# Retention attention and two MLPs on one core: a longer run of loads in flight, and one turn's matmuls in another order

## The chip, the cores and the metric

The kernel runs on one core of one Trainium2 chip. The metric is the device time of one execution in microseconds (us): the median over several runs, lower is better. A profiled execution of the same program gives the trace from which all rows below come; its times count from the start of its span.

## The reference: what is computed

Three stages follow each other. The input has batch 4, 8 heads, 576 positions and 64 features a head.

```python
scores = scale * np.matmul(q, k.transpose(0, 1, 3, 2))
Dmat = np.where(rel >= 0, gamma[:, None, None] ** rel[None, :, :], 0.0)   # causal decay, one rate a head
x = np.matmul(scores * Dmat, v)            # then (tokens, heads*64): 2304 x 512
...
h = x @ w_in;  g = np.maximum(h, 0.0) + alpha * np.minimum(h, 0.0)
x = g @ w_out                              # 512 -> 2048 -> 512
...
h = x @ w2_in; g = h * (1.0 / (1.0 + np.exp(-1.702 * h)))
out = g @ w2_out                           # 512 -> 2048 -> 512
```

## The kernel before, in words

**Attention** takes the heads in 16 pairs (4 batches by 4 pairs of heads), one pair a turn of the loop over `i`, 17 turns in all. A pair needs 1728 columns of 128 partitions in float32 (tile `ld`: queries, keys, values) and 512 columns of the keys in their other layout (tile `kts`). One column of 128 partitions is 512 bytes, so a pair is 2240 columns or 1.15 MB. The positions go in blocks of 128: products within a block (`a_scores` into PSUM tile `sc`, masked and decayed by VectorE in `a_evac`, then `a_within` with the values into PSUM tile `av`), and states that carry the decayed sum of outer products of keys and values from block to block (`a_outer` and `a_tail` into PSUM tile `st`, `a_states` on ScalarE, `a_sums` on VectorE, `a_across` into `av`). `a_keys` scales the keys of the next pair on ScalarE. In turn `i` TensorE computes the scores, the outer products and the tail of pair `i`, and the products with the values (`a_within`, `a_across`) of pair `j = i - 1`. The tile `av` has two buffers; `a_rests` on VectorE (a line of the helper `sub`, L109) is the last reader of a buffer before it is used again.

**Loads.** All loads of attention are issued by SyncE (SP), which works strictly in order. `a_load(i + 4)` stands at the end of turn `i`; `ld` has five buffers. Between them stand the loads of the first MLP's weights, which come as rows `m` of 1 MB, each in two pieces of 1024 columns (0.52 MB, tile `raw`): the rows 0, 1 and 2 lie between the loads of attention, rows 3, 4 and 5 behind them. Every one of these loads goes through `paced`: before it is issued, it waits for the landing of an earlier load, the latest one from which on at least `FLYING` columns have been issued. The unit is one column.

```python
for other, n in reversed(flying):
    behind += n
    if behind >= FLYING:
        tc.add_manual_dep(ins.ins, other.ins.name, SYNC, reason="transfers on their way")
        break
```

Each load signals its landing on one of eight semaphores, DMAHW0 to DMAHW7, which are handed out in turn; a wait on a semaphore is a wait for the load that had it last.

**The weights** are 64-bit words that are turned into float32 on chip: `w_sat` (L150), `w_range` (L154) and `w_top` (L158) on ScalarE, `w_low` (L165) on VectorE, then each is split into a high and a low part (`w_hi` L104, `w_lo` L109). A list of times (`at`, `run_to`) says in which turn each of these instructions is put into its engine's queue; the queues then run in order, so an instruction that waits for a piece of weights holds up what stands behind it on its engine.

**The first MLP** (`mm1` L532 into `h`, `mm2` L573 into `acc`) begins right behind attention, and **the second** (L714) behind it. Every product is made of three matmuls over high and low parts.

Of the kernel before, what the change touches and what calls it, by code (L numbers as in the profile page):

```python
# [39 lines left out]
NG = 5  # L40
SUM = {1: 0, 2: 1, 4: 2, 5: 3}
RING = ("w6", "X1", "w15", "X2", "X4")
FLYING = 2300
HOME = (0, 7, 2, 3, 4, 5, 6, 15)


# [1 line left out]
def kernel(  # L48
# [68 lines left out]
    def run_to(time):  # L117
        while events and events[0][0] <= time:
            _, _, fn, args = events.pop(0)
            fn(*args)  # L120
# [9 lines left out]
    def paced(out, in_, size):  # L130
        ins = nc.sync.dma_start(out=out, in_=in_)  # L131
        behind = 0
# [4 lines that stand above are left out]
# [213 lines left out]
    def a_tables(p):  # L350
        def table(o, c0, n, row, key):
            nc.vector.scalar_tensor_tensor(
                out=tab_sb[o, p, c0:c0 + n], in0=row, scalar=vtab_sb[o, p, key:key + 1],
                in1=mask_sb[o, o.start:o.start + n], op0=ALU.mult, op1=ALU.mult,
            )

        for e in range(2):
            table(slice(0, 128), e * 128, 128, query(p, e), e)
        for e, o in enumerate(halves):
            table(o, 256, 64, query(p, e, o, 64), 4)  # L360

    def a_otab(p):
        for e, o in enumerate(halves):
            copy(tab_sb[o, p, 320:448], query(p, e, o))
        o = tab_sb[:, p, 320:768]
        copy(o[:, 128:256], o[:, 0:128])
        copy(o[:, 256:448], o[:, 0:192])

    def mm(out, lhsT, rhs, start, stop):
        return nc.tensor.matmul(  # L370
            out=out, lhsT=lhsT, rhs=rhs, start=start, stop=stop, skip_group_check=True
        )

    def a_keys(i):
        n = kts(i).rearrange("p (j n) -> p j n", j=4)
        for e, o in enumerate(halves):
            scale(n[:, :, o], n[:, :, o], vtab_sb[:, PAIRS[i][1], e:e + 1])
        k_t[i] = n

    def a_scores(i, chunks=range(4)):  # L380
        q, k = ld[i][0:2]
        if i not in sc_t:
            sc_t[i] = [aps.tile([128, 512], F32, tag="sc", name="sc", bufs=3) for _ in halves]
        t = sc_t[i]
        for j in chunks:
            for h in halves:
                for e, o in enumerate(halves):
                    mm(t[e][h, j * 128:j * 128 + 128], k[j][o, h], q[j][o], j == 0, True)

    def a_tail(i):  # L390
        q, k = ld[i][0:2]
        for o in halves:
            mm(s_t[i][o, 0:64], k[4][o], q[4][o], i == 0, True)

    def a_outer(i):
        t, v, n = s_t[i], ld[i][2], k_t.pop(i)
        for j in range(4):
            for e, o in enumerate(halves):
                mm(t[o, j * 64 + 64:j * 64 + 128], n[:, j, o], v[:, 2 * j + e], i > 0 and j == 0, True)

    def a_evac(i):
        for e, t in enumerate(sc_t.pop(i)):
            nc.vector.tensor_tensor(  # L403
                out=r_t[i][0][:, e].rearrange("p (j n) -> p j n", j=4),
                in0=t.rearrange("p (j n) -> p j n", j=4),
                in1=tab_sb[:, PAIRS[i][1], e * 128:e * 128 + 128].rearrange(
                    "p (a n) -> p a n", a=1).to_broadcast([128, 4, 128]),
                op=ALU.mult,
            )

    def a_queries(i):
        behind = latest[0]
        r = tmp("r", i, [128, 2048])
        r_t[i] = (
            r[:, 0:1024].rearrange("p (e n) -> p e n", e=2), r[:, 1024:1536],
            r[:, 1088:1600].rearrange("p (b n) -> p b n", b=2)[:, :, 0:64], r[:, 1600:2048],
        )
        ins = nc.gpsimd.tensor_tensor(
            out=r_t[i][3], in0=ld[i][3], in1=tab_sb[:, PAIRS[i][1], 320:768], op=ALU.mult
        )  # L420
        if behind:
            tc.add_manual_dep(ins.ins, behind.ins.name, SYNC, reason="beside the products of the scores")

    def a_states(i):
        p = PAIRS[i][1]
        s = r_t[i][1]
        scale(s[:, 0:320], s_t.pop(i)[:, 0:320], vtab_sb[:, p, 2:3])

    def a_sums(i):
        p = PAIRS[i][1]  # L430
        s = r_t[i][1]
        nc.vector.scalar_tensor_tensor(
            out=s[:, 320:512], in0=s[:, 64:256], scalar=vtab_sb[:, p, 2:3], in1=s[:, 128:320],
            op0=ALU.mult, op1=ALU.add,
        )
        half = r_t[i][2]
        nc.vector.scalar_tensor_tensor(
            out=s[:, 384:512].rearrange("p (b n) -> p b n", b=2), in0=half,
            scalar=vtab_sb[:, p, 3:4], in1=s[:, 384:512].rearrange("p (b n) -> p b n", b=2),
            op0=ALU.mult, op1=ALU.add,  # L440
        )
        latest[0] = nc.vector.tensor_tensor(
            out=s[:, 0:64], in0=s[:, 0:64], in1=tab_sb[:, p, 256:320], op=ALU.mult
        )

    def a_within(i):
        v, r = ld[i][2], r_t[i][0]
        t = aps.tile([128, 1024], F32, tag="av", name="av", bufs=2)
        av_t[i] = t, [t[:, A0 + j * 128:A0 + j * 128 + 128] for j in range(4)] + [t[:, A0 + 512:A0 + S]]
        for j in range(4):  # L450
            for e, o in enumerate(halves):
                mm(av_t[i][1][j][o], v[:, 2 * j + e], r[:, e, j * 128:j * 128 + 128], j % 2 == 0, True)

    def a_across(i):
        out, v = av_t[i][1], ld[i][2]
        _, s, _, q = r_t.pop(i)
        for c in range(1, 5):
            s0 = 64 if c == 1 else 192 + c * 64
            for o in halves:
                mm(out[c][o], s[o, s0:s0 + 64], q[o, c * 128 - 128:min(c * 128, 448)], False, True)  # L460
        for o in halves:
            mm(out[4][o], v[o, 8], s[o, 0:64], False, True)

    def a_out(i):
        b, p = PAIRS[i]
        t = av_t.pop(i)[0][:, A0:A0 + S]
        ld.pop(i)
        s0 = 0
        for c in range(2):
            n0, n1 = max(CH[c][0] - b * S, 0), min(CH[c][1] - b * S, S)  # L470
            if n0 >= n1:
                continue
            if (c, p) not in x_t:
                x_home(c, p, xp[c])
            o = b * S - CH[c][0]
            x = x_t[c, p][:, :, n0 + o:n1 + o]
            copy(x[:, 0], t[:, n0:n1])
            rests.append((x, t[:, n0:n1]))
            s0 = n1
        if s0 < S:  # L480
            n = i - NP
            if n // 3 not in xs_t:
                xs_t[n // 3] = tmp("xs", n // 3, [128, 3, S])
            copy(xs_t[n // 3][:, n % 3, s0:S], t[:, s0:S])
# [3 lines left out]
    def a_rests():  # L488
        while rests:
            x, t = rests.pop(0)  # L490
            sub(nc.vector, x[:, 1], t, x[:, 0])
# [452 lines left out]
    with tc.manual_schedule():  # L944
# [24 lines left out]
        for i in range(n_a + 1):  # L969
            j = i - 1  # L970
            if i < n_a:
                a_scores(i)
                a_queries(i)
                a_evac(i)
            if i in (1, 2):
                a_tables(i + 1)
            a_rests()
            run_to(i)
            if i < n_a:
                s_t[i] = aps.tile([128, 512], F32, tag="st", name="st")  # L980
                if i == 0:
                    a_tail(i)
                a_outer(i)
                if i == 0:
                    a_states(i)
                    a_tables(1)
            if i != 1:
                a_within(max(j, 0))
            if 0 < i < n_a:
                a_tail(i)  # L990
                a_states(i)
            if i < n_a:
                a_sums(i)
            if i + 1 < n_a:
                a_keys(i + 1)
            if i == 0:
                a_otab(1)
            run_to(i + 0.25)
            if i:
                a_across(j)  # L1000
                a_out(j)
            if i in (1, 2):
                a_otab(i + 1)
            for n in (3, 4) if i == 0 else (i + 4,):
                if n < n_a:
                    a_load(n)
            if i == 0:
                nc.sync.dma_start(out=alpha_sb, in_=alpha)
            run_to(i + 0.75)
# [173 lines left out]
```

## Time and profile before

| | us |
|---|---|
| median of 3 runs | 815.01 |
| lowest and highest | 814.62, 815.68 |
| the profiled execution, its own time | 813.96 |
| its span in the trace | 812.3 |
| busy time of TensorE in it (98%) | 795.7 |
| mean granted TensorE clock, share of full speed | 0.995 |

The span is what the trace shows from the first to the last instruction; 1.66 us of the profiled execution's own time lie around it. Attention takes the first 79.7 us, the first MLP begins there. TensorE is busy nearly all of the time; "busy" covers slow matmuls too, so the places to look at are the waits.

### The profile page before, as it was taken

The numbers are of one execution on the slowest core, as the hardware profiler recorded it, in microseconds if no ns is written. First come the engines' busy times: TensorE is split into PE (matmuls) and PEld (weight loads), VectorE is DVE, ScalarE is ACT, GpSimd is POOL, SyncE is SP. The second block draws the span as 40 slices with busy tenths as digits, with TensorE's granted clock in tenths as the row PEclk, the third lists the DMA queues.
The fourth block names the chain that finished last, engine by engine and source line by source line (L and its number), as shares of the span: only waits on it lengthen the run. The fifth ranks groups of instructions, "written<-read, shape, count | busy, mean of one in ns | idle before, by whom it ended". The sixth has DMA issues, their size and how long they took to land.

```text
span 812.3 us, 14660 instructions
## 1 busy us (share of the span) xinstructions
PE 795.7 (98%) x5260; PEld 740.2 (91%) x5260; DVE 643.2 (79%) x1195; ACT 528.1 (65%) x959; POOL 82.3 (10%) x104
## 2 busy tenths in 40 slices
PE   8879999999999999999999999999999999999998
PEld 7767788888888888899999999999999999999998
DVE  6757897889765676878998899799787799777775
ACT  6557977888454676546577767666566676566553
POOL 2322120100001211534300000000000000000000
PEclk9989999999999999999999999999999999999999
DMA  8989999876579987598899756987544986446881
GB/s 288 317 281 324 368 322 355 329 284 234 197 263 363 398 287 248 166 316 307 277 370 333 257 161 203 336 303 261 160 120 138 358 291 222 145 122 211 290 274 64
DMA packets 89663, 214.11 MB, mean 264 GB/s; under 512 B 8179, under 2 KB 44019, under 8 KB 80886
## 3 DMA queue, kind: packets, MB, share of 16 engines
q1 hardware_dynamic: 82656, 187.99, 66.1%
q0 software_dynamic: 6784, 25.17, 9.1%
q8 instruction: 41, 0.67, 0.3%
q14 instruction: 32, 0.26, 0.1%
q10 hardware_dynamic: 150, 0.02, 0.0%
HBM read 152.59 MB, written 60.56 MB: 262 GB/s over the span
## 4 chain that ended last, share of the span: by engine, by line
PE 87%; DMA 10%; ACT 2%; SPq 1%; DVE 0%; issue 0%; DVEq 0%
PE acc L714 32%; PE h L714 25%; PE acc L573 15%; PE h L532 14%; DMA raw<-in_w_dram 5%; DMA ld<-in_qkv_dram 3%; DMA kts<-in_kn_dram 1%; SPq L131 0%; ACT raw L150 0%; ACT raw L158 0%; ACT gsf L104 0%; ACT g L545 0%; DVE raw L195 0%; DVE r L403 0%; ACT raw L154 0%
## 5 line engine op out<-in xcount | busy, mean ns | idle before, releaser
L109 DVE TENSOR_TENSOR gsf<-g,gsf 128x384 fp32r<-128x384 f32 (+1 forms) x272 | 157.0, 590 | 54.2 <-ACT gsf L104 53.0
L104 ACT ACTIVATE gsf<-g 128x384 fp32r<-128x384 f32 (+1 forms) x272 | 145.8, 542 | 74.7 <-PE acc L714 33.0
L573 PE MATMUL acc<-gsf,wo 128*128 128x512 f32 x576 | 138.5, 390 | 0.9 <-ACT gsf L104 0.6
L532 PE MATMUL h<-x,wi 128*128 128x512 f32 x576 | 138.2, 389 | 0.0
L714 PE MATMUL acc<-gsf,ws 128*128 128x384 f32 x768 | 135.0, 334 | 0.0
L714 PEld LDWEIGHTS acc<-gsf,ws 128*128 128x128 f32 x768 | 133.3, 188 | 0.0
L573 PEld LDWEIGHTS acc<-gsf,wo 128*128 128x128 f32 x576 | 107.9, 188 | 24.5 <-ACT gsf L104 1.0
L532 PEld LDWEIGHTS h<-x,wi 128*128 128x128 f32 x576 | 108.0, 188 | 22.5
L714 PE MATMUL acc<-x,ws 128*128 128x384 f32 x660 | 128.2, 334 | 0.0
L714 PEld LDWEIGHTS acc<-x,ws 128*128 128x128 f32 x660 | 115.6, 188 | 0.0
L714 PE MATMUL h<-x,ws 128*128 128x384 f32 x540 | 107.7, 334 | 0.0
L714 PE MATMUL h<-gsf,ws 128*128 128x384 f32 x576 | 101.8, 334 | 0.0
L714 PEld LDWEIGHTS h<-gsf,ws 128*128 128x128 f32 x576 | 100.0, 188 | 0.0
L714 PEld LDWEIGHTS h<-x,ws 128*128 128x128 f32 x540 | 94.8, 188 | 0.0
L195 DVE TENSOR_TENSOR tm<-h,tm 128x384 f32<-128x384 f32 x97 | 53.7, 554 | 26.9 <-PE h L714 21.5
L195 DVE TENSOR_TENSOR g<-g 128x384 f32<-128x384 f32 x114 | 63.3, 555 | 0.7
L540 DVE SCALAR_TENSOR_TENSOR g<-g,rise_sb,h 128x512 f32<-128x512 f32 (+1 forms) x49 | 36.4, 743 | 31.7 <-ACT g L545 31.5
L104 ACT ACTIVATE tm<-acc 128x384 f32<-128x384 f32 x62 | 30.4, 491 | 47.4 <-PE acc L714 45.8
L545 ACT ACTIVATE g<-h 128x512 f32<-128x512 f32 (+1 forms) x49 | 29.0, 592 | 39.8 <-PE h L532 39.2
L195 DVE TENSOR_TENSOR raw<-raw 128x256 f32<-128x256 f32 x116 | 45.7, 435 | 1.0
L150 ACT ACTIVATE raw<-raw 128x1024 f32<-128x1024 f32 x32 | 36.5, 1141 | 14.4 <-DMA raw<-in_w_dram 11.0
L165 DVE SCALAR_TENSOR_TENSOR raw<-raw 128x1024 int32<-128x1024 int32 x32 | 39.4, 1231 | 2.7 <-ACT raw L158 2.6
(104 smaller groups left out, 915.8 us busy)
## 6 DMA issues: line engine op xcount, KB each, us to landing
ws<-sm SPq DMA_DIRECT2D x32, 1024.0 KB, 6.8
ws<-sp SPq DMA_DIRECT2D x24, 1024.0 KB, 5.5
raw<-in_w_dram POOLq DMA_DIRECT2D x44, 512.0 KB, 7.9
sm<-raw SPq DMA_DIRECT2D x32, 512.0 KB, 4.3
pad<-rg SPq DMA_DIRECT2D x48, 256.0 KB, 2.7
ld<-in_qkv_dram SPq DMA_DIRECT2D x26, 432.0 KB, 4.7
raw<-in_w_dram SPq DMA_DIRECT2D x20, 512.0 KB, 7.4
r<-raw SPq DMA_DIRECT2D x16, 512.0 KB, 3.0
```

The costliest lines, as they stand in the source:

```text
L104: return nc.scalar.activation(out=out, in_=in_, func=ACTF.Copy)
L109: latest[0] = eng.tensor_tensor(out=out, in0=a, in1=b.bitcast(F32), op=ALU.subtract)
L150: nc.scalar.activation(out=f, in_=f, func=IDENTITY_SAT240, scale=2.0 ** -9)
L165: latest[0] = nc.vector.scalar_tensor_tensor(out=g[:, 0:2 * DM], in0=t[:, :, 1], scalar=3, in1=t[:, :, 0], op0=ALU.logical_shift_left, op1 ...
L195: latest[0] = (eng or nc.vector).tensor_tensor(out=out, in0=x, in1=y, op=op)
L532: nc.tensor.matmul(out=t, lhsT=w[:, cw, k * 128:k * 128 + 128], rhs=x[:, cx], start=(i == 0), stop=(i == 3 * NK - 1),)
L540: nc.vector.scalar_tensor_tensor(out=g[0], in0=g[1], scalar=rise_sb[:, m:m + 1], in1=h, op0=ALU.mult, op1=ALU.add)
L545: nc.scalar.activation(out=out, in_=in_, func=ACTF.Relu, scale=-1.0)
L573: nc.tensor.matmul(out=acc[0][d], lhsT=w[:, d // 2, cw, d % 2 * 128:d % 2 * 128 + 128], rhs=g[:, cx], start=(m == m0 and i == 0), stop=(m ...
L714: nc.tensor.matmul(out=out, lhsT=w(cw), rhs=x(cx), start=(start and n == 0), stop=True, skip_group_check=True,)
```

## The change

`FLYING` goes from 2300 columns (1.18 MB) to 3500 (1.79 MB). In the fourth turn (`i == 3`) the products of pair 2 with its values (`a_within`) are put ahead of the outer products of pair 3.

```diff
-FLYING = 2300
+FLYING = 3500
...
                 if i == 0:
                     a_tail(i)
+                if i == 3:
+                    a_within(j)
                 a_outer(i)
                 if i == 0:
                     a_states(i)
                     a_tables(1)
-            if i != 1:
+            if i not in (1, 3):
                 a_within(max(j, 0))
             if 0 < i < n_a:
                 a_tail(i)
```

On SP no load is moved; what changes is the load for which each one waits. This is the stretch around the two pieces of row 1 of the weights (`raw_577`), with the second half of pair 10 (the second `ld_641`); the numbers tell tiles apart. Before:

```order
L131 DMA raw_577<-in_w1_dram 128x1024 [waits DMAHW0_49]
L131 DMA ld_641<-in_qkv_dram 128x864 [waits DMAHW2_49,PE_49,Pool_49]
L131 DMA kts_126<-in_kn_dram 128x512 [waits DMAHW3_49,Activation_49]
L131 DMA ld_641<-in_qkv_dram 128x864 [waits DMAHW4_49]
L131 DMA raw_577<-in_w1_dram 128x1024
L131 DMA ld_708<-in_qkv_dram 128x864 [waits DMAHW1_49,DMAHW6_49,PE_49,Pool_49]
```

And the same loads with the change:

```order
L131 DMA raw_577<-in_w1_dram 128x1024 [waits DMAHW7_49]
L131 DMA ld_641<-in_qkv_dram 128x864 [waits DMAHW0_49,PE_49,Pool_49]
L131 DMA kts_126<-in_kn_dram 128x512 [waits DMAHW1_49,Activation_49]
L131 DMA ld_641<-in_qkv_dram 128x864 [waits DMAHW2_49]
L131 DMA raw_577<-in_w1_dram 128x1024 [waits DMAHW3_49]
L131 DMA ld_708<-in_qkv_dram 128x864 [waits DMAHW4_49,PE_49,Pool_49]
```

DMAHW4 is the semaphore of the first piece of `raw_577`, DMAHW2 and DMAHW3 those of the two loads ahead of it (`kts` and the second half of `ld` of pair 9). So the second half of pair 10 waited for the piece of weights, with 864 + 512 = 1376 columns (0.70 MB) issued behind that piece; now it waits for the `kts` of pair 9, with 864 + 1024 + 864 + 512 = 3264 columns (1.67 MB) issued behind it. Among loads of attention alone it was 2240 columns (1.15 MB), and is 2752 or 3104 (1.41 or 1.59 MB).

On TensorE the fourth turn reads so (`st<-ld,kts` are the outer products, `av<-r,ld` the products with the values):

```order
 L370 MATMUL sc<-ld 64x128 x16
-L370 MATMUL st<-ld,kts 64x64 x8
-L370 MATMUL av<-r,ld 64x128 x8
+L370 MATMUL av<-r,ld 64x128 x8
+L370 MATMUL st<-ld,kts 64x64 x8
 L370 MATMUL st<-ld 64x64 x2
```

The eight products with the values of pair 2 stand ahead of the eight outer products of pair 3; nothing else moves on any engine.

## Rows read from the trace of the kernel before

**Rows 1.** The page: its first line.

```profile
span 812.3 us, 14660 instructions
```

**Rows 2.** Waits of TensorE over the run: us in total, times, longest.

```profile
PE sc L370 <- DMA ld<-in_qkv_dram: 6.7, 7, 2.0
PE st L370 <- ACT kts L334: 2.8, 1, 2.8
...
PE acc L573 <- ACT gsf L104: 0.6, 1, 0.6
...
PE acc L573 <- ACT raw L104: 0.4, 1, 0.4
```

**Rows 3.** The chain that ended last, in order of time: start, us, what.

```profile
39.83 5.96 DMA raw<-in_w_dram
...
66.77 4.06 DMA ld<-in_qkv_dram
...
70.88 0.74 PE sc L370 x16
...
77.41 9.62 DMA raw<-in_w_dram
...
100.59 2.97 PE acc L573 x12
```

**Rows 4.** Waits of SP's queue, 0 to 80 us: us in total, times, longest.

```profile
SPq L131 <- DMA ld<-in_qkv_dram: 21.4, 24, 2.6
SPq L131 <- DMA kts<-in_kn_dram: 16.0, 15, 2.5
SPq L131 <- DMA raw<-in_w_dram: 9.2, 6, 2.6
```

**Rows 5.** Windows: busy time by engine; last three columns: clock, DMA share, GB/s.

```profile
10.00:20.00 10.00, 9.46 (x220) 8.17 (x218) 8.29 (x21) 7.89 (x24) 2.44 (x3) 1.00 0.95 314
2.00:51.00 49.00, 42.15 (x886) 35.87 (x885) 33.43 (x78) 29.15 (x70) 11.41 (x10) 0.99 0.92 309
...
2.00:71.00 69.00, 57.87 (x1226) 49.74 (x1229) 45.30 (x104) 43.80 (x97) 17.16 (x15) 0.95 0.91 305
80.00:110.00 30.00, 29.06 (x126) 23.07 (x125) 23.96 (x38) 27.36 (x38) 2.29 (x4) 1.00 1.01 372
44.00:48.00 4.00, 3.35 (x74) 2.79 (x72) 3.38 (x7) 1.37 (x4) 1.14 (x1) 1.00 0.76 230
```

**Rows 6.** Timeline of SP's queue, 42 to 46 us: start, us, what.

```profile
42.64 0.58 SPq L131 DMA_DIRECT2D kts<-in_kn_dram  x1
45.81 0.33 SPq L131 DMA_DIRECT2D ld<-in_qkv_dram  x1
```

**Rows 7.** Timeline of TensorE: pieces of attention that waited, wait in brackets.

```profile
34.40 0.67 PE L370 MATMUL sc<-ld 64*64 64x128 f32 x16 [1.00 <-DMA ld<-in_qkv_dram]
...
39.85 0.67 PE L370 MATMUL sc<-ld 64*64 64x128 f32 x16 [1.34 <-DMA ld<-in_qkv_dram]
...
53.34 1.41 PE L370 MATMUL st<-ld,kts 128*64 128x64 f32 x15 [2.80 <-ACT kts L334]
...
68.83 0.67 PE L370 MATMUL sc<-ld 64*64 64x128 f32 x16 [0.55 <-DMA ld<-in_qkv_dram]
70.88 0.67 PE L370 MATMUL sc<-ld 64*64 64x128 f32 x16 [1.39 <-DMA ld<-in_qkv_dram]
```

**Rows 8.** Timeline of ScalarE around 51 us.

```profile
51.38 1.10 ACT L150 ACTIVATE raw<-raw 128x1024 f32<-128x1024 f32 x1 [6.00 <-DMA raw<-in_w_dram]
```

**Rows 9.** Timeline of TensorE in the fourth turn.

```profile
18.48 0.69 PE L370 MATMUL st<-ld,kts 128*64 128x64 f32 x16
19.71 1.09 PE L370 MATMUL av<-r,ld 128*64 128x128 f32 x16 [0.54 <-DVE x L109]
```

**Rows 10.** Timeline of TensorE in the first MLP.

```profile
88.76 3.29 PE L573 MATMUL acc<-gsf,wo 128*128 128x512 f32 x12 [0.57 <-ACT gsf L104]
```

**Rows 11.** Line L131 (the paced loads), 0 to 72 us: issue to landing.

```profile
DMA to landing us min/median/max: 2.7/4.7/6.2
```

## The prediction

> **What bounds the kernel now.** I began with the waits of TensorE over the whole run [rows 2]. They fall into two places. Nearly all stand in attention: 6.7 us for the scores' operands to land and 2.8 us for keys that ScalarE had not yet scaled. Behind attention only 0.6 and 0.4 us are left, both where the first MLP begins. From there on nothing stops TensorE, so whatever is won or lost by 100 us should reach the end unchanged. That confines the question to the first eighth of the span [rows 1].
>
> The chain that ended last says what sets that part. It reaches TensorE's unbroken work at 100.59 us and before that goes through transfers: the load of pair 14's second half, issued at 66.77 and landed 4.06 us later, releases the scores at 70.88; a piece of weights issued at 77.41 takes 9.62 us to land and feeds the first MLP [rows 3]. The reader should see that in between stands SP: each load was issued when another had landed. SP's own waits confirm it: 21.4 + 16.0 + 9.2 = 46.6 us in which it held a load back for an earlier one [rows 4]. The pacing by columns is such a wait.
>
> Then the windows, for whether the 16 DMA engines had work meanwhile. From 2 to 71 us they were busy 0.91 of the time at 305 GB/s; from 80 to 110 us, where many transfers are on their way, 1.01 at 372 GB/s; from 10 to 20 us, where the stream has no weights in it yet, 0.95 [rows 5]. So while the core waits for transfers, the engines idle 69 x 0.09 = 6.2 us.
>
> The timelines show where. In the stretch quoted with the change, SP issues `kts` at 42.64 and the next load only at 45.81 [rows 6], when the piece of weights issued at 39.83 has landed, at 45.79 [rows 3]. Only 0.70 MB had been issued behind that piece. The window 44 to 48 us falls to a share of 0.76 and 230 GB/s [rows 5]: 0.96 us of idle engines. The weights bring six such pieces into the stream, which are the six waits for `raw` in SP's list [rows 4].
>
> **The change part by part.**
>
> *The pacing.* It adds no instruction and no byte and moves no load. It shortens the holds. In front of the load that is awaited there were 2240 columns among attention's loads and 1376 behind a piece of weights; now 2752 to 3264, at both places more than in the best of the old stretches. What is that worth? The stretch from 2 to 71 us holds 69 x 0.91 = 62.8 us of work for the engines. The least gain is none, if the idle share comes from something else than the holds. At 0.95, the share of 10 to 20 us with 2240 columns in front, it would last 66.1 us: 2.9 us less. At 1.0 it would last 62.8: 6.2 us less. I take 0.96, close to the row with the same sort of loads and a little above it, because more stands in front than there: 62.8 / 0.96 = 65.4, so the load of pair 14 lands **3.6 us** earlier. I leave the rate per busy engine as it is (305 / 0.91 = 335 GB/s), though the later stretch shows 368.
>
> A page can be held against this. The hole at 44 to 48 us shows 0.96 us lost behind 0.70 MB, and 10 to 20 us shows 0.05 of the time lost behind 1.15 MB [rows 5]. The Trainium skill, DMA: Bandwidth & Descriptors (Anatomy of one DMA), gives a transfer a fixed part of about 2.0 us, most of it the receipt of the last write, and beyond it bytes over 436 GB/s, fitted on transfers issued by GpSimd. By that page 0.70 MB cover 1.6 us of the 2.0 and leave 0.4 us, six times 2.4 us, and 1.15 MB leave nothing; its estimate of the gain is 2.4 us. The trace agrees on the kind, and shows more idle time at both depths.
>
> *Whether TensorE can follow.* Pair 14 waited 0.55 + 1.39 = 1.94 us for its two halves [rows 7]; without them it would have been ready at 70.88 - 1.94. What held it further up is in turn 10: ScalarE stood 6.00 us at 51.38 for the second piece of weights row 1 [rows 8], the scaling of the keys was queued behind, and the outer products waited 2.80 us for that, to 53.34 [rows 7]. That piece also moves: the window 2 to 51 us, 49 us at 0.92 [rows 5], gives 49 x (1 - 0.92 / 0.96) = 2.0 us. So TensorE can follow by 1.94 + 2.0 = 3.9 us, just more than the 3.6 us that the load gives. At a share of 1.0 the two bounds are 6.2 and 49 x 0.08 + 1.94 = 5.9 us; the latter is the upper bound of the gain.
>
> *Behind attention.* At 70.88 the scores release VectorE, which releases stores and then SP's next loads, up to the weights' piece of 77.41 [rows 3]. All of that is counted from 70.88 and moves with it. The engines are full there, so the 9.62 us stay. In the first MLP TensorE waited 0.57 us for work queued behind that piece on ScalarE [rows 10], so this landing has to move as far as attention does; I take that it does. The bound below is that it does not move, and then only the 0.57 and 0.4 us of waiting are gained.
>
> *The fourth turn.* Eight outer products (0.69 us) stood between the scores and the products with the values, and these still waited 0.54 us for the last reader of their `av` buffer on VectorE [rows 9]. Turned round, the products with the values start at the same 19.71, since VectorE sets that, and the outer products follow instead of filling the wait: at most 0.69 us later. If the scaled keys of pair 3 came late the turn would save something, but before they were ready by 18.48. What covers the 0.69 us is TensorE's later waits for loads: 1.00 us at 34.40 and 1.34 at 39.85 [rows 7]. With loads 38 x (1 - 0.92 / 0.96) = 1.6 us earlier by then, 2.34 - 1.6 = 0.74 us of wait is left, just enough. Price: nothing; 0.69 us if the loads get faster than I take, and then it lies in the part that the 6.00 us of ScalarE sets anyway.
>
> *Sum.* 0 for the order, -3.6 us for the pacing. The profiled execution took 813.96 us, of which 812.3 are span [rows 1]; 813.96 - 3.6 = 810.4. It lies 1.05 us below the median of the runs, 815.01, to which the forecast is made: **811.4 us**.
>
> **The rivals.**
>
> *The engines are fuller, the bytes no faster.* The idle share may come from slow packets or from engines that finish unevenly, so that the slowest has no idle time now and more in front adds only queueing. For it: from 10 to 20 us, with steady depth, 0.95 still gave only 314 GB/s [rows 5], hardly more than the mean of 305. Against it: the clear hole behind the weights' piece and the 372 GB/s with more on the way. Then no landing moves: 815.0.
>
> *Won in attention, given back at the first MLP.* The piece of weights of 77.41 needs 9.62 us in a stretch where the engines are full [rows 3]. If that stretch is bound by its bytes from further back than SP's issue, it lands when it did, and TensorE waits longer at 88.76. Gain 0.57 + 0.4 us [rows 2, 10]: 814.0. Against it: before 80 us the engines still had gaps.
>
> *Slower: what is needed now shares the engines with what is needed later.* If transfers on their way divide the bandwidth and don't land in the order of their issue, more of them make each one later. Landing took 4.7 us in the median with about 2240 + 864 columns on the way [rows 11]; with 3104 + 864 it takes 4.7 x 3968 / 3104 = 6.0. The chain has two such landings that decide, pair 14's and the weights' piece behind it, so 2 x 1.3 = 2.6 us: 817.6. It decides once the longer landing exceeds what the earlier issue gives, 1.3 us each. For it: the 9.62 us of the piece where most is on its way [rows 3]. Against it: in that same stretch the rate is the best of all [rows 5], and 4.7 us is about the time that everything in front takes, which tells nothing of the order. On the page named above, Latency and other measured facts lets the access of HBM go from 0.2 us to 2 us under high load, which would make landings later too; no run here shows it by itself.
>
> **How the numbers follow.** About 0.2% (1.6 us) is what a measurement of this kernel can tell from no change. Forecast (0.96, down to 0.95 and up to full engines): 0.66. No faster bytes: 0.17. Given back: 0.08. Slower: 0.09. The forecast's own range is 815.0 - 5.9 = 809.1 to 815.0 - 2.9 = 812.1. The two cases without a change have 0.25 together, so the range must take them in: up to 815.2, and down to 809.0. The slower case stays outside. Faster by over 0.2% (under 813.4) is the forecast alone, 0.66; the same, 0.25; slower, 0.09.
>
> **What would show it.** Right: the share of the DMA engines from 2 to 71 us rises to 0.95 or more; no gap of 3 us in SP's issues behind a piece of weights; the scores of pair 14's second half start at about 67.3 instead of 70.88; the piece of weights for the first MLP lands near 83.4; TensorE's unbroken work begins near 97. In the fourth turn the products with the values wait about 1.2 us and start near 19.7. Wrong: a higher share at the same 305 GB/s, or pair 14 still at 70 us; landings of 6 us with later scores in the first turns; a wait of 3 to 4 us in place of the 0.57 at the first MLP; or a new wait of ScalarE or SP for buffers that takes the place of the wait for loads.

## The result, and the profile after

The changed kernel takes 806.83 us in the median (806.68 to 807.13, 4 runs) against 814.9 us (814.62 to 815.68, 4 runs): a ratio of 0.99, 95% interval 0.9883 to 0.9917, or 8.1 us less. The forecast of 811.4 us had the direction and the mechanism, but less than half of the size, and the time lies below the range that began at 809.0.

The page's first line, of the changed kernel; the span is 7.3 us shorter than in [rows 1]:

```profile
span 805.0 us, 14657 instructions
```

The waits of TensorE over its run (us in total, times, longest) answer to [rows 2]. The 6.7 us of waiting for the scores' operands are gone in this execution, and so are the 0.6 and 0.4 us where the first MLP begins; the 0.2 us for ScalarE in the list stand much later, at 256 us. What remains in attention behind the fourth turn is the wait for scaled keys, 2.5 us, and two short waits for nothing that the profile shows ("issue"), which stood nowhere before:

```profile
PE st L370 <- ACT kts L334: 2.5, 1, 2.5
...
PE av L370 <- DVE x L109: 0.8, 1, 0.8
PE av L370 <- issue: 0.8, 1, 0.8
PE sc L370 <- issue: 0.5, 1, 0.5
PE acc L573 <- ACT gsf L104: 0.2, 1, 0.2
```

The windows of the changed kernel, last three columns clock, DMA share and GB/s, beside [rows 5]: the share from 2 to 71 us is 1.00 where it was 0.91, at 356 GB/s where it was 305. From 10 to 20 us, without any weights, the rate rises from 314 to 359. The window 44 to 48 us held a hole of 0.24 and is full, though other loads lie in it now:

```profile
10.00:20.00 10.00, 9.23 (x201) 7.92 (x199) 8.21 (x21) 7.21 (x22) 2.43 (x3) 1.00 0.99 359
2.00:51.00 49.00, 44.80 (x924) 39.18 (x925) 35.57 (x83) 32.80 (x76) 12.61 (x11) 0.97 1.00 356
2.00:71.00 69.00, 63.56 (x1375) 55.79 (x1376) 52.13 (x121) 47.87 (x103) 18.37 (x16) 0.98 1.00 356
44.00:48.00 4.00, 1.36 (x30) 0.79 (x22) 1.23 (x5) 2.43 (x5) 0.00 (x0) 0.92 1.01 383
```

SP's queue shows how. In the stretch quoted with the change `kts` is issued at 37.15 and the next load 0.69 us later, where it was 3.17 us [rows 6]:

```profile
37.15 0.33 SPq L131 DMA_DIRECT2D kts<-in_kn_dram  x1
37.84 0.33 SPq L131 DMA_DIRECT2D ld<-in_qkv_dram  x1
```

The lead grows along the stream. The second half of pair 14 was issued at 66.77 and the first MLP's piece of weights at 77.41 [rows 3]; now it is 11.7 and 11.6 us earlier:

```profile
55.05 1.48 SPq L131 DMA_DIRECT2D ld<-in_qkv_dram  x2
65.83 2.78 SPq L131 DMA_DIRECT2D raw<-in_w_dram  x3
```

SP still waits for landings, 37.2 us in 0 to 80 us instead of 46.6 [rows 4]; that is no loss as long as the engines have work meanwhile:

```profile
SPq L131 <- DMA ld<-in_qkv_dram: 25.0, 30, 2.6
SPq L131 <- DMA raw<-in_w_dram: 8.9, 8, 1.7
...
SPq L131 <- DMA kts<-in_kn_dram: 3.3, 11, 0.5
```

The timeline of TensorE, the places with a wait in the second half of attention, beside [rows 7]. The scores of pairs 7, 8, 10 and 14 no longer wait for loads; the outer products of the eleventh turn (the prediction's turn 10) start at 47.53 instead of 53.34:

```profile
47.53 1.41 PE L370 MATMUL st<-ld,kts 128*64 128x64 f32 x15 [2.52 <-ACT kts L334]
63.85 0.32 PE L370 MATMUL sc<-ld 64*64 64x128 f32 x1 [0.49 <-issue]
70.41 0.86 PE L370 MATMUL av<-r 64*64 64x128 f32 x12 [0.75 <-issue]
```

And of ScalarE, whose wait for the second piece of weights row 1 lies ahead of that, beside [rows 8]:

```profile
45.57 1.10 ACT L150 ACTIVATE raw<-raw 128x1024 f32<-128x1024 f32 x1 [3.13 <-DMA raw<-in_w_dram]
```

The first MLP begins at 73.49 instead of 79.7, and the product that began TensorE's unbroken work at 100.59 [rows 3] begins at 92.79:

```profile
73.49 8.46 PE L532 MATMUL h<-x,wi 128*128 128x512 f32 x36
81.79 2.88 PE L573 MATMUL acc<-gsf,wo 128*128 128x512 f32 x12
...
92.79 2.52 PE L573 MATMUL acc<-gsf,wo 128*128 128x512 f32 x10
```

So of the 7.3 us, 6.2 come in attention (79.69 to 73.49). From the start of the first MLP to that product it was 20.9 us and is 19.3: 1.6 us more. Together 7.8; half a microsecond is lost again further on. The median moved by 0.8 us more than the profiled executions did, because the profiled one of before (813.96) lay below its median.

### The profile page after: what moved, and what is told of

It is laid out like the page before. It is cut to its first block, busy times and chain, and to the rows that moved or that the text cites. A ratio compares the mean times of both kernels' runs of the same rounds, so it can differ in the third digit from the quotient of the medians.

```text
span 805.0 us, 14657 instructions
## 1 busy us (share of the span) xinstructions
PE 794.8 (99%) x5260; PEld 740.8 (92%) x5260; DVE 643.2 (80%) x1195; ACT 527.6 (66%) x959; POOL 82.4 (10%) x104
## 4 chain that ended last, share of the span: by engine, by line
PE 87%; DMA 2%; DVE 2%; SPq 1%; ACT 1%; issue 1%; POOLq 0%; DVEq 0%; ACTq 0%
PE acc L714 33%; PE h L714 25%; PE acc L573 13%; PE h L532 13%; PE av L370 2%; DMA rg<-raw 1%; DMA raw<-in_w_dram 1%; PE st L370 1%; PE sc L370 1%; SPq L515 1%; DVE raw L215 1%; DMA x<-part 0%; DVE g L540 0%; DVE gsf L109 0%; ACT gsf L104 0%
```

## Experiments

The theory: the longer run of loads keeps the DMA engines full, and that is all of the gain; the fourth turn's order brings nothing. The rivals: the order is needed for it; or the holes behind the pieces of weights alone count; or more on the way makes what is needed first late. Every ratio below is to the kernel before on the same chip.

**The two parts apart.** The pacing alone:

```diff
-FLYING = 2300
+FLYING = 3500
```

> Pacing at 3500 columns, the fourth turn in its old order. Theory (the longer run of loads fills the DMA engines, and that is the whole of the gain): 806.3 to 807.1 us, 0 to 0.5 us less than with both, since the outer products fill a wait again (products with the values of the fourth turn wait about 0.3 us). Rival (the turned order is needed, since the scaled keys of pair 3 come too late with more loads on the way): 808 us or more, with a wait of the outer products of the fourth turn for keys of over 1 us.

Measured: 808.12 us (805.29 to 808.99, 5 runs), ratio 0.9898, 0.9881 to 0.9916, the same as with both parts. Its window, the pacing alone:

```profile
2.00:71.00 69.00, 63.21 (x1364) 55.11 (x1363) 52.24 (x120) 48.13 (x103) 18.35 (x16) 0.95 0.99 355
```

The median lies 1 us above the expectation, inside the spread of its runs. The wait for keys in the fourth turn that the rival needs does not exist. The order alone:

```diff
+                if i == 3:
+                    a_within(j)
...
-            if i != 1:
+            if i not in (1, 3):
```

> The turned fourth turn at the old pacing of 2300 columns. Theory: 814.9 to 815.6 us, nothing gained, and at most the 0.69 us of the outer products lost; the share of the DMA engines from 2 to 71 us stays at 0.91. Rival (the order brings part of the 8 us): 813 us or less.

Measured: 814.86 us, ratio 0.9995, 0.9983 to 1.0008: no change, and the engines as idle as before:

```profile
2.00:71.00 69.00, 58.26 (x1222) 50.18 (x1221) 45.77 (x104) 42.49 (x94) 16.53 (x15) 0.95 0.91 301
```

The pacing carries the gain.

**Which part of the run: behind the weights, or everywhere.** Both kernels have the old order. In the first a piece of weights counts nothing, which closes the holes behind it and, among attention's loads, changes nothing else:

```diff
-            paced(out, in_, 1024)
+            paced(out, in_, 0)
```

> Pacing at 2300 columns and the old order, but the pieces of weights are not counted, so that behind a piece at least 2240 columns of attention are in front, as elsewhere. It closes the holes behind the weights and leaves the rest. Theory (both the holes and the short run elsewhere left engines idle): 810 to 811 us, share of the DMA engines 2 to 71 us near 0.96. Rival 1 (the holes are all of it): 807 us and a share of 0.99. Rival 2 (the holes cost nothing, the run elsewhere is all): 814 us or more.

Measured: 812.68 us, ratio 0.9964, 0.9947 to 0.9981. The window that had the hole is full, the whole stretch is not:

```profile
2.00:71.00 69.00, 60.67 (x1276) 52.40 (x1277) 46.89 (x107) 44.70 (x97) 17.29 (x15) 0.93 0.93 318
44.00:48.00 4.00, 3.16 (x74) 2.68 (x70) 3.55 (x8) 1.67 (x5) 1.14 (x1) 1.00 1.02 367
```

The second half of pair 14 is issued 5.1 us earlier than the 66.77 of [rows 3]:

```profile
61.69 1.91 SPq L131 DMA_DIRECT2D ld<-in_qkv_dram  x2
```

The complement leaves the waits around a piece among attention's loads as they were and lengthens the others:

```diff
-FLYING = 2300
+FLYING = 3500
...
-            paced(out, in_, 1024)
+            paced(out, in_, 2124)
```

> The complement: 3500 columns among attention's loads, but a piece of weights counts as 2124 columns, so that the loads around a piece wait for the same loads as before. Old order. Theory (both count): 811 to 812 us, share near 0.94. Rival 1 (the holes behind the weights are all): 814.5 us or more. Rival 2 (the run elsewhere is all): 807 us.

Measured: 811.92 us, ratio 0.9953, 0.9939 to 0.9967. Here the stretch without weights is full and the whole again is not:

```profile
10.00:20.00 10.00, 9.26 (x241) 8.46 (x242) 9.82 (x28) 8.09 (x24) 3.42 (x3) 1.00 1.00 361
2.00:71.00 69.00, 60.29 (x1301) 52.15 (x1304) 47.54 (x110) 45.27 (x99) 17.18 (x15) 0.95 0.92 317
```

The second half of pair 14 is issued 2.9 us earlier than before:

```profile
63.89 1.40 SPq L131 DMA_DIRECT2D ld<-in_qkv_dram  x2
```

Both rivals fall: each edit brings the stream forward, and neither by the 11.7 us of both together. 0.36% and 0.47% come to 0.83%, against 1.02% with both in the pacing alone: the parts add up roughly, and neither is the whole. The first was 1.7 us short of its expectation.

The split of the time is rough for two reasons. Both edits also reach the pieces of rows 3 to 5, which follow each other behind attention: the first lets many more of them go out at once, the second leaves 1024 columns in front where it was 2048. In the profiles the first kernel reaches the first MLP 0.6 us earlier (79.13 for 79.69) and, like the changed kernel, gains another 1.6 us by the product that began the unbroken work (98.42 for 100.59); the second gains 1.9 us in attention (77.80), of which 1.7 are left at that product (98.91). And single executions differ: from 10 to 20 us the first kernel still has the same loads and the same holds as before, but its share was 0.85 where [rows 5] have 0.95.

**A shorter and a much longer run.** Before, with 1600 columns:

```diff
-FLYING = 2300
+FLYING = 1600
```

> Before, with the pacing at 1600 columns. Theory (the run of loads sets how full the DMA engines are): the share from 2 to 71 us falls from 0.91 to about 0.8, the rate to 260 GB/s or less; TensorE waits for loads throughout and the time rises to 823 us or more. Rival (only the stretch behind the weights counts, and 1376 columns are left elsewhere too): within 2 us of before.

Measured: 833.34 us, ratio 1.0217, 1.0197 to 1.0238, which is 18 us more where the rival allows 2. Share, rate and TensorE's wait for loads, two views:

```profile
2.00:71.00 69.00, 50.34 (x988) 42.40 (x989) 37.88 (x87) 35.49 (x81) 13.08 (x12) 0.90 0.76 246
```

```profile
PE sc L370 <- DMA ld<-in_qkv_dram: 19.3, 13, 3.7
```

The changed kernel with 6000 columns:

```diff
-FLYING = 3500
+FLYING = 6000
```

> The changed kernel with the pacing at 6000 columns, where the eight landing semaphores set the limit. Theory (at 3500 the engines are full, and TensorE is held by its own chain): 806 to 808 us, share 1.0 and 355 GB/s as at 3500. Rival (a longer run makes what is needed first land later): 809 us or more, with waits of the first turns for loads.

Measured: 807.89 us (806.29 to 810.99), ratio 0.9913, 0.9886 to 0.994; no difference to 3500 can be told. The rate does rise further, and TensorE waits neither for loads nor, in the eleventh turn, for scaled keys. Yet it gains nothing by that; instead it stands 2.7 us at the scores for something that the profile does not show, and the first MLP begins at 73.02:

```profile
2.00:71.00 69.00, 63.73 (x1384) 55.46 (x1383) 51.66 (x119) 47.80 (x103) 18.41 (x16) 0.98 1.01 381
```

```profile
PE sc L370 <- issue: 2.7, 2, 2.4
```

The first turns did not get later, so the rival of late landings falls. The theory's "355 GB/s as at 3500" was wrong too: 381.

**Where the last 1.6 us come from.** The changed kernel, with rows 3 to 5 of the weights, which stand behind attention's loads, paced as before:

```diff
-            paced(out, in_, 1024)
+            paced(out, in_, 1024, FLYING if key[1] < 3 else 2300)
```

(the last argument of `paced` takes the place of `FLYING` in it).

> The changed kernel, with the weights rows 3, 4 and 5 behind attention's loads paced at 2300 columns as before. Theory 1 (the weights of the first MLP land early because the whole stream is early): same as the changed kernel, 806.5 to 807.3 us, first MLP without waits. Theory 2 (the longer run behind attention gives the last 1.6 us): 808 to 808.6 us, with waits of about 1 us for ScalarE at the first MLP.

Measured: 806.76 us, ratio 0.9899, 0.9875 to 0.9923, and TensorE has no wait for ScalarE at the first MLP, whose first three products start at 73.76, 82.05 and 84.84. The pacing of rows 3 to 5 themselves is not what gave the 1.6 us; the weights are in time because the whole stream is ahead.

**What binds now.** The changed kernel, ScalarE's passes over weights row 1 later:

```diff
-        (1, "raw0", (5.5, 6.5), (8.75, 9.75, 10.75, 12.0), 12.25, 13.0),
+        (1, "raw0", (5.5, 6.5), (9.75, 10.75, 11.25, 12.0), 12.25, 13.0),
```

> The changed kernel, with ScalarE's first pass over weights row 1 put one turn later (and the two next ones behind it), so that ScalarE doesn't stand for the piece ahead of the scaling of pair 10's keys. Theory (TensorE's wait of 2.52 us in the eleventh turn, and the slow clock behind it, are what now binds attention): 803 to 805 us, the wait gone, the granted clock of 44 to 51 us at full speed. Rival (the loads of pairs 13 and 14 or VectorE bind just behind): 806 us or more.

Measured: 805.81 us (804.34 to 806.78), ratio 0.9881, 0.9862 to 0.9901. The wait of 2.52 us is gone and the first MLP begins 4.0 us earlier still; pair 14 waits for its loads again:

```profile
60.71 0.67 PE L370 MATMUL sc<-ld 64*64 64x128 f32 x16 [1.44 <-DMA ld<-in_qkv_dram]
69.53 8.48 PE L532 MATMUL h<-x,wi 128*128 128x512 f32 x36
```

That it is more than the wait has to do with TensorE's clock. Behind the wait, from 48 to 50 us, the changed kernel's granted clock was 0.50, the lower level of 1.2 GHz, and from these outer products to the next turn's it took 5.21 us (47.53 to 52.74) where the turn behind takes 3.52 (52.74 to 56.26). Without the wait the clock stays at 2.4 GHz. From 44 to 51 us, the changed kernel and then this one:

```profile
44.00:51.00 7.00, 4.36 (x64) 3.46 (x56) 2.49 (x6) 3.90 (x6) 1.15 (x1) 0.76 1.02 371
```

```profile
44.00:51.00 7.00, 6.97 (x174) 6.04 (x170) 4.63 (x12) 5.60 (x10) 2.30 (x2) 1.00 1.02 380
```

But the span is only 2.4 us shorter (802.6). The second MLP begins 4.2 us earlier (331.24 for 335.46) and lasts 471.4 us to the end of the span instead of 469.5; a wait of TensorE appears there that the changed kernel's profile does not have:

```profile
PE h L714 <- DMA ws<-r: 0.8, 1, 0.8
```

The time lies between the theory (up to 805) and the rival (from 806), and the intervals of this and the changed kernel overlap, so it is not shown to be faster. The rest was an attempt to have both, with one chip for three kernels: the changed kernel again, then with the later passes and 4500 columns, then this with the old order of the fourth turn.

```diff
-FLYING = 3500
+FLYING = 4500
...
-                if i == 3:
-                    a_within(j)
...
-            if i not in (1, 3):
+            if i != 1:
```

(the last four lines in the third kernel only).

> The changed kernel once more, for comparison on the same chip as the next two: 806.5 to 808 us.

> The changed kernel with ScalarE's passes over weights row 1 a turn later, and the pacing at 4500 columns. Theory (with the eleventh turn's wait gone, what held TensorE were the loads of pairs 13 and 14, by 1.8 us; a longer run brings these early): TensorE's waits for loads gone, first MLP begins at 68 to 69 us, 803.5 to 805 us. Rival (what is won in front is given back in the second MLP, in waits for its weights): first MLP early, but 805.5 us or more.

> The same with the fourth turn in its old order. Theory (the turned order costs up to 0.69 us where no later wait covers it): 0.2 to 0.7 us less than with the turned order, the first MLP that much earlier. Rival (the order decides nothing, another engine sets the pace of the turns): within 0.2 us.

Measured: 806.48 us (803.99 to 809.8; ratio 0.9866 to 0.9916), 807.92 us (805.74 to 809.31; 0.9878 to 0.9922) and 804.95 us (801.98 to 810.44; 0.9836 to 0.9907). The intervals overlap; the runs of one kernel lie up to 8.5 us apart here, and which of the three is fastest stays open, and with it the price of the order where nothing covers it. The 4500 columns did not bring the first MLP to 68 or 69 us, as the theory had it and the rival too: it begins at 73.97. TensorE stood 1.17, 0.79 and 3.21 us for nothing that the profile shows, the last at one matmul of pair 14's scores:

```profile
63.91 0.32 PE L370 MATMUL sc<-ld 64*64 64x128 f32 x1 [3.21 <-issue]
```

The changed kernel's second profile shows how far two executions of one kernel differ. It still waits for the scores' operands, has none of the short unexplained waits, and reaches the first MLP at 72.13 instead of 73.49; but its second MLP lasts 471.4 us instead of 469.5, and its span is 805.3:

```profile
PE sc L370 <- DMA ld<-in_qkv_dram: 1.6, 2, 1.2
```

Over all the profiles here the second MLP lasts 469.5 to 471.4 us, not in step with when it begins, and that hides what the last variants are worth.

## Why the prediction was off

*Idle DMA engines while the core waits for transfers, caused by the pacing:* right. Pacing alone has the gain, 1600 columns lose 2.2%, and both places named, behind the weights and elsewhere, count.

*The term of the sum, 62.8 / 0.96 = 65.4, "close to the row with the same sort of loads and a little above it":* mis-sized, and this is the step that failed. The share became 1.00, and the load of pair 14 is issued 11.7 us earlier where the term let it land 3.6 us earlier. The row of 10 to 20 us that I leaned on was itself held down by the pacing: the same window went from 0.95 to 0.99.

*"I leave the rate per busy engine as it is (335 GB/s), though the later stretch shows 368":* wrong as well. It became 356 / 1.00. The 69 x 305 GB/s = 21.0 MB of that stretch take 59.1 us at 356 GB/s, so by the rates alone the stream came forward by 9.9 us. The row of 80 to 110 us had said so.

*TensorE can follow by 3.9 and at most 5.9 us:* the path was right, with a piece of weights as the limit, but its terms were not. The piece had 2.0 us, at most 3.9, from the same share at an unchanged rate; ScalarE's pass moved from 51.38 to 45.57 and the outer products from 53.34 to 47.53, 5.8 us both. The 1.94 us of pair 14's waits went as well, which makes 7.8; the new waits of 0.49 and 0.75 us and some 0.3 us more took part of it back, and the first MLP came 6.2 us earlier. That the bound of 5.9 lies so close is luck. The clock has no visible part in the 6.2: behind the eleventh turn's wait it was granted at 0.50 (1.2 GHz) in both kernels, from 51 to 56 us before and from 48 to 50 now, and from those outer products to the next turn's it took 5.19 us before (53.34 to 58.53) and 5.21 now (47.53 to 52.74).

*Behind attention, "I take that it does" move as far:* too small by 1.6 us. The weights' piece was issued 11.6 us earlier and attention ended 6.2 us earlier, so the waits of 0.57 and 0.4 us that I had counted as staying went, and the product of 88.76 [rows 10], now at 81.79, takes 2.88 us instead of 3.29.

*The fourth turn, price nothing:* right as far as it can be told. The products with the values start at 19.75, where 19.71 was expected, and waited 0.77 us. The order alone gives 0.9995.

*The rivals:* fuller engines with no more bytes: no, 305 became 356 GB/s. Given back at the first MLP: the opposite. Landings too late: a load takes longer from issue to landing (below), but it is issued earlier by more. The page's estimate, DMA: Bandwidth & Descriptors (Anatomy of one DMA) of the Trainium skill, 2.4 us for the holes behind the weights alone, comes near the 0.36% (2.9 us) of the kernel that closes these (and lengthens the run of rows 3 to 5); that 1.15 MB leave nothing, as the prediction worked it out from there, the complement's 0.47% contradicts.

## What to carry to other kernels

Where loads are held back by the bytes in front of them, look at what is left behind the load that is awaited, not at the limit: one large piece in the stream left 0.70 MB here where the limit said 1.18. For the size of a gain take the fullest stretch of the trace, its share and its rate, as the end of the range that is likely, and not a stretch that the same limit holds down. Then look for the next in-order wait, since it decides how much of it the core can use: here a wait of ScalarE for weights took over. At 6000 columns that wait was gone too, but waits that the profile does not explain stood in its place, and the higher rate brought nothing that can be told.

## What the runs showed of the hardware

The rate per busy engine rises with the run of loads: from 2 to 71 us 246 / 0.76 = 324 GB/s at 1600 columns, 335 at 2300, 356 at 3500 and 381 / 1.01 = 377 at 6000. That is not only because other loads come into the window: from 10 to 20 us, where all four move attention's loads, it is 240 / 0.76 = 316, 331, 363 and 407 / 1.04 = 391. The two ends:

```profile
10.00:20.00 10.00, 6.76 (x133) 6.12 (x125) 6.57 (x15) 5.26 (x16) 2.29 (x2) 0.83 0.76 240
```

```profile
10.00:20.00 10.00, 9.21 (x234) 8.09 (x228) 9.57 (x26) 7.18 (x22) 3.18 (x3) 1.00 1.04 407
```

A share below one therefore understates what was to be had here.

Each load takes longer, and TensorE waits for loads less all the same. Issue to landing of line L131 from 0 to 72 us had a median of 4.7 us [rows 11]; the same row at 1600, at 3500 and at 6000 columns:

```profile
DMA to landing us min/median/max: 2.5/4.0/6.3
```

```profile
DMA to landing us min/median/max: 2.7/5.6/10.7
```

```profile
DMA to landing us min/median/max: 2.6/6.6/8.9
```

With the engines full, TensorE stands now and then for nothing that the profile shows. At the same place, one matmul of pair 14's scores, it was 0.49 us in the changed kernel, 2.38 at 6000 columns, and 3.21 with 4500 columns and the later passes, where it stood from 60.70 to 63.91 (above). There the DMA queues in 61.5 to 62.6 us (packets, MB, share) hold a transfer of instructions:

```profile
q1 hardware_dynamic: 162, 0.41, 95.2%
q8 instruction: 1, 0.02, 5.4%
```

That TensorE waited for these instructions, which by this view share the engines with the loads, fits the place and is no more than a guess; it was not tried.
